# Attention and MLP in one kernel: Q and K rows interleaved in DRAM, and steps of the evacuation in other slots

## The chip, the cores and the metric

The kernel runs on one NeuronCore of a Trainium2 chip. The metric is the device time of one execution in microseconds (us). Times below are of the kernel before the change unless the text says otherwise. Six names recur. PE is the matmul engine, PEld its weight loads, DVE the vector engine, ACT the scalar engine, POOL the GpSimd engine, and SP the engine whose queue issues every DMA of this kernel. Each of them works through its own list of instructions in order. An instruction that waits holds up everything behind it on the same engine.

## The reference

The input is one sequence of 2048 rows of 512 numbers. The rows are layer-normalized; the normalized rows feed an attention block of 32 heads of width 16 and a dense block of width 1792, and the two results are combined.

```python
xn = _layernorm(x, axis=-1)
# A: attention, H = 32 heads, Dh = 16
q, k, v = (xn @ wqkv).reshape(B, S, 3, H, Dh) ...
scores = jnp.einsum("bhqd,bhkd->bhqk", q, k) * (Dh ** -0.5)
o = jnp.einsum("bhqk,bhkd->bhqd", _softmax(scores, axis=-1), v)
s = o.transpose(0, 2, 1, 3).reshape(B, S, D) @ wo
# B: dense, F = 1792
r = jnp.where(h > 0, h, 0)        # h = xn @ w1 + b1
b = (r * r) @ w2 + b2
return x + s * _silu(b)
```

Most products are made from numbers split in a high and a low part, three partial products each (high-high, high-low, low-high), so that the result keeps more bits than one pass would.

## The kernel before

**Lead-in (0 to about 196 us).** The rows are loaded, normalized and transposed. The Q, K and V projections run on PE. Q and K go out to DRAM tiles `q_d` and `k_d` of shape `[2, 128, 2048]`: index 0 of the first axis holds the high parts of 128 rows (8 heads of 16), index 1 the low parts. They come back later in another arrangement. For one head, 48 partitions of a tile `qe`, `qm` or `ka` hold three groups of 16 rows, for Q high, high, low and for K high, low, high, so that one matmul over 48 rows adds the three partial products. Each group is one DMA: three loads a head, for two heads (`j`) a tile.

**The loop.** Everything else is a loop of 512 slots. A unit is 16 slots: 4 heads and 512 queries. Unit u owns slots 16u to 16u+15, and in slot `st` PE computes the scores of 128 keys for the 4 heads of its unit (L1256, tile `se`), ACT takes the exponent (L1262, tile `pt`), and two slots later PE multiplies the exponents with V into the bank `po` (L373, 8 weight loads a slot; the last V column is 1, so that row 16 of each head is the sum). Rows `po L373` of the trace thus count the slots.

**The maxima.** The exponents need a shift for each query. Ahead of its use, the kernel computes the scores of a later unit once more (L300, tile `pm_t`, from `qm`), and DVE takes the maximum of each bank (L308): 2048 such reductions, 64 a unit. When a unit has all its maxima, `max_end` reduces them (L326), and `shift` negates them and splits the result: L336 makes the high part, L337 the low part, L341 transposes. The result goes to DRAM (`keep`, L344) and from there into two rows of the `qe` tiles (`back`, L364). From unit 16 on this happens about 7 slots ahead of the unit that needs it.

**The evacuation of a unit.** When a unit's `po` is complete, in slot 16u+17, ACT copies it to `ot`, and six steps follow at the slot distances of the table `EVAC` (`EVAC_LAST` for the last units): `evac_sums` (SP, loads the four rows of sums into a small tile `sm`), `evac_recip` (DVE, L397), `evac_keep` (SP, to DRAM `r_d`), `evac_back` (SP, broadcast back to `hl`), `evac_norm` (POOL, three operations, L411 to L413), `evac_store` (SP, four DMAs to `on_d`).

**The dense work.** PE has room beside the scores. A generator `dense` hands out its items a slot, or a block of four slots (`long_slots`), at a time: the MLP in 8 chunks of 256 rows (`mlp_tasks`: `first`, `first_pair`, `second`), then the output projection (`wo_part`) in blocks of 128 rows `(c, tt)`, four slots each, in the order `WO_ORDER`. Blocks of the columns c = 2 and 3 of the sequence, which wait for the last two units, are computed without those and finished at the very end (`unit_inner`, `unit_final`, `fill_mms`, `run_fill`). The tile `oc` holds the attention output that a column of blocks reads; `wo_load` and `wo_load_last` fill it.

**What sets the order.** Inside the loop the order on ACT, DVE, POOL, SP and PE is the order in which the Python code emits the instructions. `begin(st)` emits what is due in a slot: loads of K and V for the next four heads, loads of `qe` for the next unit, and then everything that `later(n, ...)` had put off to this slot. Loads of `qm` are emitted by `max_end` at steps counted in maxima (16 steps a unit).

Of the kernel before, what the change touches and what calls it, by code (L numbers as in the profile page):

```python
# [16 lines left out]
P = 128  # L17
# [17 lines left out]
EVAC = (1, 4, 5, 7, 9, 12)  # L35
EVAC_LAST = (1, 3, 4, 5, 7, 9)
# [4 lines left out]
def kernel(  # L41
# [16 lines left out]
    q_d = [dram.tile([2, P, S], F32, name=f"q_d{m}") for m in range(4)]  # L58
    k_d = [dram.tile([2, P, S], F32, name=f"k_d{m}") for m in range(4)]
# [12 lines left out]
    nc.vector.memset(eps_t, EPS)  # L72
    b1_t = const.tile([P, FO], F32, name="b1_t")
# [22 lines left out]
    with ExitStack() as ph:  # L96
# [33 lines left out]
        def load_head(t, j, src_d, h, parts, cols):  # L130
            for n, i in enumerate(parts):
                nc.sync.dma_start(  # L132
                    t[64 * j + DH * n : 64 * j + DH * (n + 1), :].bitcast(F32),
                    src_d[h // 8][i, (h % 8) * DH : (h % 8 + 1) * DH, cols],
                )

        def load_k(qd, n):

            p, j, i = n // 6, n // 3 % 2, n % 3
            if n % 6 == 0:  # L140
                kas[qd, p] = ring("ka")
            h = 4 * qd + 2 * p + j
            nc.sync.dma_start(
                kas[qd, p][64 * j + DH * i : 64 * j + DH * (i + 1), :].bitcast(F32),
                k_d[h // 8][i % 2, (h % 8) * DH : (h % 8 + 1) * DH, :],
            )
# [20 lines left out]
        def load_q_pair(u, name, p, tiles):  # L167
                qd, qc = divmod(u, 4)
                t = ring(name)
                for j in range(2):  # L170
                    load_head(
                        t, j, q_d, 4 * qd + 2 * p + j, (0, 0, 1), slice(qc * 512, (qc + 1) * 512)
                    )
# [140 lines left out]
        def max_end():  # L314
            while steps[0] < sum(done_m) // 4:
# [6 lines left out]
                if s in (9, 11) and u + 1 < NU:  # L322
                    load_q_pair(u + 1, "qm", (s - 9) // 2, qms.setdefault(u + 1, []))
# [10 lines left out]
        def shift(u):  # L334
            sh = sp.tile([P, 2, 16], F32R, name="sh")
            nc.vector.tensor_scalar(sh[:, 0], mxs[u], -1.0, None, op0=ALU.mult)  # L336
# [14 lines left out]
            if in_loop:  # L351
                later(1, keep)
                later(max(2, 16 * u - 14 - now[0]), back)
            else:
# [3 lines left out]
                else:  # L358
                    waiting.append((16 * u - 14, back))
# [19 lines left out]
        def evac(po, u):  # L379
# [4 lines left out]
            steps = EVAC_LAST if u >= 28 else EVAC  # L384
# [40 lines left out]
        def mlp_tasks(mp):  # L425
# [7 lines left out]
            rp = m1.enter_context(tc.tile_pool(name="rp", bufs=1))  # L433
# [119 lines left out]
            def second(c, tt):  # L553
# [86 lines left out]
        def wo_setup():  # L640
            wp = right(wstk, "wop", 1)
            st = right(wstk, "wo_st", 2)
# [6 lines left out]
            for ko in range(KO):  # L649
                later(3 * ko, lambda ko=ko: load(ko))  # L650
            wos["w"] = wot

# [843 lines left out]
```

## Time and profile before

| | us |
|---|---|
| median of 3 runs | 1661.2 (1657.56 to 1661.68) |
| the profiled execution | 1662.81 |
| its span | 1661.0 |
| lead-in, to the first `po` of the loop | about 196 |
| loop and tail | about 1465 |

Busy shares of the span: PE 98%, DVE 81%, ACT 72%, PEld 59%, POOL 31%. A busy PE does not mean that it is at its peak: matmuls overlap and their ends are modelled. The chain of waits, followed back from the last instruction, lies on PE for 93%. So the profile is best read slot by slot: two neighbouring slots of the same make-up take the same time to about 0.05 us, and a slot that is longer than its like shows a wait.

### The profile page before, as it was taken

The numbers are of one execution on the slowest core, as the hardware profiler recorded it, in microseconds if no ns is written. First come the engines' busy times: TensorE is split into PE (matmuls) and PEld (weight loads), VectorE is DVE, ScalarE is ACT, GpSimd is POOL, SyncE is SP. The second block draws the span as 40 slices with busy tenths as digits, with TensorE's granted clock in tenths as the row PEclk, the third lists the DMA queues.
The fourth block names the chain that finished last, engine by engine and source line by source line (L and its number), as shares of the span: only waits on it lengthen the run. The fifth ranks groups of instructions, "written<-read, shape, count | busy, mean of one in ns | idle before, by whom it ended". The sixth has DMA issues, their size and how long they took to land.

```text
span 1661.0 us, 35806 instructions
## 1 busy us (share of the span) xinstructions
PE 1625.6 (98%) x13642; PEld 983.6 (59%) x13642; DVE 1349.1 (81%) x2332; ACT 1187.8 (72%) x2344; POOL 510.9 (31%) x533
## 2 busy tenths in 40 slices
PE   6999999999999999999999999999999999998998
PEld 4899666456656665665565456555655565544455
DVE  6499888888887788877888888888888888887833
ACT  6221487678877887887787777777777777776784
POOL 4435567513212221231133113201321224113224
PEclk9999999999999999999999999999999999999999
DMA  8677555426332522353243324342332442144344
GB/s 285 168 227 251 176 173 165 124 65 175 85 91 74 164 74 81 101 138 73 78 122 98 92 72 140 93 109 72 116 98 71 106 127 73 45 117 128 124 134 140
DMA packets 155924, 201.22 MB, mean 121 GB/s; under 512 B 54824, under 2 KB 73768, under 8 KB 154216
## 3 DMA queue, kind: packets, MB, share of 16 engines
q1 hardware_dynamic: 155752, 198.93, 41.1%
q8 instruction: 108, 1.77, 0.4%
q14 instruction: 64, 0.52, 0.1%
HBM read 144.58 MB, written 53.99 MB: 120 GB/s over the span
## 4 chain that ended last, share of the span: by engine, by line
PE 93%; DVE 3%; DMA 2%; SPq 1%; ACT 0%; issue 0%; POOL 0%; DVEq 0%; ACTq 0%
PE po L373 29%; PE pm_t L300 16%; PE pd_t L234 16%; PE se L1256 15%; PE pd_t L202 5%; PE se L1014 3%; DVE mx L308 2%; PE se L965 2%; PE pd_t L773 2%; PE pd_t L1014 1%; PE po L1014 1%; SPq L132 1%; DMA sm<-ot 0%; DMA xc<-xn_d 0%; DMA xt<-in_A_x_dram 0%; PE pm_t L807 0%
## 5 line engine op out<-in xcount | busy, mean ns | idle before, releaser
L308 DVE TENSOR_REDUCE mx<-pm_t 128x1 f32<-128x512 f32 x2048 | 1265.4, 682 | 220.3 <-PE pm_t L300 120.8
L1262 ACT ACTIVATE pt<-se 128x512 f32<-128x512 f32 x1750 | 928.1, 613 | 234.7 <-PE se L1256 152.6
L300 PE MATMUL pm_t<-ka,qm 64*128 64x512 f32 x2048 | 783.1, 418 | 12.4 <-DVE mx L308 11.2
L1256 PE MATMUL se<-qe,ka 64*128 64x512 f32 x2016 | 745.0, 415 | 0.1
L373 PE MATMUL po<-pt,v 128*32 128x512 f32 x3564 | 525.3, 603 | 0.0
L300 PEld LDWEIGHTS pm_t<-ka,qm 64*128 64x128 f32 x2048 | 359.9, 184 | 227.0 <-DVE mx L308 214.0
L1256 PEld LDWEIGHTS se<-qe,ka 64*128 64x128 f32 x2016 | 353.3, 184 | 113.2 <-ACT pt L1262 74.1
L234 PEld LDWEIGHTS pd_t<-xc,w1s 64*128 64x128 f32 x2352 | 296.1, 187 | 44.2 <-issue 41.9
L234 PE MATMUL pd_t<-xc,w1s 64*128 64x256 f32 x2352 | 322.0, 286 | 0.0
L234 PE MATMUL pd_t<-w2t,hT 64*128 64x512 f32 x936 | 254.3, 407 | 0.0
L373 PE MATMUL po<-ex,v 128*32 128x512 f32 x532 | 213.2, 602 | 0.0
L1262 ACT ACTIVATE ex<-se 128x512 f32<-128x512 f32 x266 | 159.0, 614 | 43.2 <-PE se L1256 22.4
L234 PEld LDWEIGHTS pd_t<-w2t,hT 64*128 64x128 f32 x936 | 159.7, 184 | 43.6 <-issue 35.2
L373 PEld LDWEIGHTS po<-pt,v 128*32 128x32 f32 x3564 | 89.2, 108 | 160.4 <-issue 146.9
L547 POOL TENSOR_TENSOR r<-r 128x512 f32<-128x512 f32 x49 | 51.0, 1041 | 322.6 <-ACT r L544 322.6
L566 POOL TENSOR_TENSOR u<-u,b_t 128x512 f32<-128x512 f32 x16 | 20.6, 1287 | 286.6 <-ACT u L565 286.6
L202 PE MATMUL pd_t<-w2t,hT 64*128 64x512 f32 x408 | 106.3, 392 | 1.6 <-POOL w2t L81 0.8
L411 POOL TENSOR_TENSOR ot<-ot,hl 128x512 f32<-128x512 f32 x31 | 39.9, 1286 | 220.9 <-DMA hl<-r_d 148.2
L202 PEld LDWEIGHTS pd_t<-w2t,hT 64*128 64x128 f32 x408 | 72.4, 184 | 11.6 <-POOL w2t L80 1.2
L773 PE MATMUL pd_t<-wot,oc 64*128 64x512 f32 x258 | 74.5, 411 | 0.0
L81 POOL TENSOR_TENSOR hT<-r,hT 128x512 fp32r<-128x512 f32 x56 | 72.3, 1291 | 4.7
L1014 PE MATMUL se<-xT,wr_t 64*128 64x512 f32 x312 | 65.9, 390 | 0.0
(130 smaller groups left out, 1202.7 us busy)
## 6 DMA issues: line engine op xcount, KB each, us to landing
w1s<-w_d SPq DMA_DIRECT2D x196, 256.0 KB
qm<-q_d SPq DMA_DIRECT2D x384, 32.0 KB
qe<-q_d SPq DMA_DIRECT2D x384, 32.0 KB
ka<-k_d SPq DMA_DIRECT2D x96, 128.0 KB
xn_d<-xT SPq DMA_DIRECT2D x8, 1024.0 KB
k_d<-hl SPq DMA_DIRECT2D x32, 256.0 KB
q_d<-hl SPq DMA_DIRECT2D x32, 256.0 KB
xc<-xn_d SPq DMA_DIRECT2D x16, 512.0 KB
```

The lines of the kernel that those rows point to most:

```text
L81: (lo or nc.gpsimd).tensor_tensor(dst[1], raw, dst[0].bitcast(F32), op=ALU.subtract)
L202: mm = nc.tensor.matmul(out_, lh(r), rh(r), start=first_ and lane == 0, stop=last_ and lane == 1, skip_group_check=True,)
L234: mm = nc.tensor.matmul(out_, lh(r), rh(r), start=first_ and lane == 0, stop=last_ and lane == 1, skip_group_check=True,)
L300: nc.tensor.matmul(ps, qms[u][p][64 * j : 64 * j + 64, qb * P : (qb + 1) * P], kas[qd, p][64 * j : 64 * j + 64, kc * 512 : (kc + 1) * 512] ...
L308: return nc.vector.tensor_reduce(mxs[u][:, c, kc : kc + 1], ps, axis=AX.X, op=ALU.max)
L373: nc.tensor.matmul(po[32 * j : 32 * j + 32, :], vs[qd][:, (4 * kb + j) * VW : (4 * kb + j) * VW + 32], pts[j], start=(kb == 0), stop=(kb = ...
L411: nc.gpsimd.tensor_tensor(ot, ot, hl[:, 1].bitcast(F32), op=ALU.mult)
L547: nc.gpsimd.tensor_tensor(r, r, r, op=ALU.mult)
L773: inst = nc.tensor.matmul(ps[lane], oc[r, a, n, ts_], wot[r, b, n], start=m == 0 and (lane == 0 or wide), stop=m == kos and (lane == 1 or ...
L1014: inst = nc.tensor.matmul(out_, lh(r), rh(r), start=first_ and lane == 0, stop=last_ and lane == 1, skip_group_check=True,)
L1256: nc.tensor.matmul(se, kas[qd, j // 2][b : b + 64, kb * P : (kb + 1) * P], qes[u][j // 2][b : b + 64, :], start=True, stop=True,)
L1262: return nc.scalar.activation(pts[j], se, AF.Exp, scale=0.25)
```

## The change

The order of rows in DRAM: `q_d` and `k_d` become `[128, 2, 2048]`, with the high and the low row of each of the 128 rows side by side (for K the low one first). Two groups of a head are then 32 neighbouring rows, and one DMA loads them; a second DMA loads the remaining 16 rows. A store of Q is one DMA in place of two.

Other slots: `EVAC` and `EVAC_LAST` have new distances, and `EVAC_LAST` holds from unit 26 on; the first `qm` pair of a unit is asked for at step 3 in place of 9; the `qe` pairs of unit u in slots 16u-11 and 16u-10 in place of 16u-16 and 16u-15; the shift rows of units whose maxima are early, in slot 16u-9 in place of 16u-14; K loads one a slot over 8 slots in place of two a slot over 6; `gate` of the MLP one slot later.

The negation L336 becomes a `scalar_tensor_tensor` with a tile of zeros as its second tensor.

The output projection begins in slot 452 in place of 456: four slots that carried no dense work are gone. The tile for its first column is loaded ahead, while the MLP ends, and is used again for column 1. One more block, (3, 2), moves from the tail into the loop, so that the blocks from (0, 0) on keep their slots.

```diff
-EVAC = (1, 4, 5, 7, 9, 12)
-EVAC_LAST = (1, 3, 4, 5, 7, 9)
+EVAC = (1, 5, 6, 8, 12, 15)
+EVAC_LAST = (1, 4, 5, 6, 8, 10)
...
-    q_d = [dram.tile([2, P, S], F32, name=f"q_d{m}") for m in range(4)]
-    k_d = [dram.tile([2, P, S], F32, name=f"k_d{m}") for m in range(4)]
+    q_d = [dram.tile([P, 2, S], F32, name=f"q_d{m}") for m in range(4)]
+    k_d = [dram.tile([P, 2, S], F32, name=f"k_d{m}") for m in range(4)]
...
-        def load_head(t, j, src_d, h, parts, cols):
-            for n, i in enumerate(parts):
+        def load_head(t, j, src_d, h, hi, cols, both):
+            r = slice((h % 8) * DH, (h % 8 + 1) * DH)
+            if both:
                 nc.sync.dma_start(
-                    t[64 * j + DH * n : 64 * j + DH * (n + 1), :].bitcast(F32),
-                    src_d[h // 8][i, (h % 8) * DH : (h % 8 + 1) * DH, cols],
+                    t[64 * j : 64 * j + 2 * DH, :].bitcast(F32),
+                    src_d[h // 8][r, :, cols].rearrange("r i n -> (r i) n"),
                 )
+            else:
+                nc.sync.dma_start(
+                    t[64 * j + 2 * DH : 64 * j + 3 * DH, :].bitcast(F32),
+                    src_d[h // 8][r, hi, cols],
+                )
...
-                if s in (9, 11) and u + 1 < NU:
-                    load_q_pair(u + 1, "qm", (s - 9) // 2, qms.setdefault(u + 1, []))
+                if s in (3, 11) and u + 1 < NU:
+                    load_q_pair(u + 1, "qm", s // 11, qms.setdefault(u + 1, []))
...
-            nc.vector.tensor_scalar(sh[:, 0], mxs[u], -1.0, None, op0=ALU.mult)
+            nc.vector.scalar_tensor_tensor(
+                sh[:, 0], mxs[u], -1.0, zero, op0=ALU.mult, op1=ALU.add
+            )
...
-                later(max(2, 16 * u - 14 - now[0]), back)
+                later(max(2, 16 * u - 9 - now[0]), back)
...
-            steps = EVAC_LAST if u >= 28 else EVAC
+            steps = EVAC_LAST if u >= 26 else EVAC
...
-                    later(2, gate)
+                    later(3, gate)
...
             wos["w"] = wot
+            wos["oc", 2] = right(wstk, "oc2p", 1).tile([P, 2, KO, 512], F32R, name="oc2")
+            later(13, lambda: wo_load(2))
+            later(21, lambda: wo_load_last(2))
...
         WO_ORDER = (
-            [(2, t) for t in range(4)] + [(3, 0), (3, 1)]
+            [(2, t) for t in range(4)] + [(3, t) for t in range(3)]
...
-            for tt in (2, 3):
-                ps = tail["ps", tt] = free_ps["w"][tt - 2]
+            for tt in (3,):
+                ps = tail["ps", tt] = free_ps["w"][0]
...
-            wo_load(2)
-            later(1, lambda: wo_load_last(2))
             wo_ask(0)
             wo_ask(1)
-            for _ in range(4):
-                yield [], None
...
-            if st >= 64 and st % 64 < 6 and st // 64 + 1 < NQ:
-                for n in range(2):
-                    load_k(st // 64 + 1, 2 * (st % 64) + n)
+            if st >= 64 and st % 64 < 8 and st // 64 + 1 < NQ:
+                load_k(st // 64 + 1, st % 64)
             u, s = divmod(st + 16, 16)
-            if 2 <= u < NU and s < 2:
-                load_q_pair(u, "qe", s, qes.setdefault(u, []))
+            if 2 <= u < NU and s in (5, 6):
+                load_q_pair(u, "qe", s - 5, qes.setdefault(u, []))
...
-        run_fill(8)
+        run_fill(1)
         tail["out"](3)
-        run_fill(5)
```

What the change moves on the engines is shown at three places. Line numbers of the changed kernel are 2 to 13 higher; the numbers behind tile names are buffers.

The first place is SP's queue at the start of unit 29, slots 464 to 467, before: `on_d<-hl` is the store of unit 27, `qe` and `qm` are the loads of queries, `sm<-ot` the sums of unit 28.

```order
L420 DMA on_d_132<-hl 16x2x512 x4
L132 DMA qe_685<-q_d_60 16x512 x6
L713 DMA g<-g_d 128x512
L718 DMA xr<-in_A_x_dram 128x512
L132 DMA qe_686<-q_d_60 16x512 x6
L132 DMA qm_201<-q_d_60 16x512 x6
L391 DMA sm<-ot 128x1x16
L132 DMA qm_199<-q_d_60 16x512 x6
```

The same place after the change, from the rows `g` and `xr` of slot 460 on.

```order
L722 DMA g<-g_d 128x512
L727 DMA xr<-in_A_x_dram 128x512
L707 DMA oc_21230<-on_d_132 64x2x512
L722 DMA g<-g_d 128x512
L727 DMA xr<-in_A_x_dram 128x512
L398 DMA sm<-ot 128x1x16
L135 DMA qm_201<-q_d_60 32x512
L140 DMA qm_201<-q_d_60 16x512
```

The 18 query loads that stood ahead of the sums are behind them or far ahead of them. On DVE the reciprocal that reads these sums stood behind 40 maxima of its unit:

```order
L341 STREAM_TRANSPOSE sq<-sh 128x32
L308 TENSOR_REDUCE mx<-pm_t 128x1 x40
L397 RECIPROCAL sm<-sm 128x16
L308 TENSOR_REDUCE mx<-pm_t 128x1 x16
L326 TENSOR_REDUCE m_22195<-mx 128x16
```

and stands behind 45 now:

```order
L348 STREAM_TRANSPOSE sq<-sh 128x32
L313 TENSOR_REDUCE mx<-pm_t 128x1 x45
L404 RECIPROCAL sm<-sm 128x16
L313 TENSOR_REDUCE mx<-pm_t 128x1 x11
L331 TENSOR_REDUCE m_21927<-mx 128x16
```

The second place is POOL in the last MLP chunk, at the normalization of unit 24, before: `r` and `hT` are the square and the split of a `first_pair` block, `ot` and `hl` the normalization.

```order
L547 TENSOR_TENSOR r_2622<-r_2622 128x512
L80 TENSOR_SCALAR hT<-r_2622 128x512
L81 TENSOR_TENSOR hT<-r_2622,hT 128x512
L411 TENSOR_TENSOR ot<-ot,hl 128x512
L412 TENSOR_SCALAR hl<-ot 128x512
L413 TENSOR_TENSOR hl<-ot,hl 128x512
L547 TENSOR_TENSOR r_2623<-r_2623 128x512
```

After, the normalization stands one block later, behind the fourth in place of the third.

```order
L554 TENSOR_TENSOR r_2577<-r_2577 128x512
L82 TENSOR_SCALAR hT<-r_2577 128x512
L83 TENSOR_TENSOR hT<-r_2577,hT 128x512
L418 TENSOR_TENSOR ot<-ot,hl 128x512
L419 TENSOR_SCALAR hl<-ot 128x512
L420 TENSOR_TENSOR hl<-ot,hl 128x512
L554 TENSOR_TENSOR r_2576<-r_2576 128x512
```

The third place is the tail on PE, before: `se` are the last products of unit 30 (L855), `pm_t` the fill (L807), `po` the V product of slot 510.

```order
L855 MATMUL se<-w_21701,hl 128x512 x9
L807 MATMUL pm_t<-wot,oc 128x512 x8
L855 MATMUL se<-w_21701,hl 128x512 x3
L807 MATMUL pm_t<-wot,oc 128x512 x5
L373 MATMUL po<-pt_1499,v_1612 32x512
```

After:

```order
L865 MATMUL se<-w_21286,hl 128x512 x9
L817 MATMUL pm_t<-wot,oc_21230 128x512
L865 MATMUL se<-w_21286,hl 128x512 x3
L380 MATMUL po<-pt_1476,v_1592 32x512
L380 MATMUL po<-pt_1468,v_1592 32x512
```

Twelve fill matmuls are gone from it; the fill of the later steps (2, 4 and 5 matmuls) stays. In slots 452 to 455 PE has 21 half-row matmuls of block (2, 0) that were not there, and the maxima of these slots stand as 5, 3, 5, 3 in place of 4 a slot. Every other slot of the loop has the same instructions on PE.

More of the change, by code (lines that the diff above doesn't have):

```diff
@@ L687, in part @@
                 )
[L689 to L694 removed]
+            for ko in range(3):
+                later(ko, lambda ko=ko: part(ko, 0, 512))
         def wo_load_last(c):
@@ L724, in wo_part @@
         def wo_part():
-            for k in range(14):
+            for k in range(15):
                 c, tt = WO_ORDER[k]
```

86 lines of the change are left out of this document (43 added, 43 removed).

## The prediction

> **What bounds the kernel now.** I read first the page's busy shares and its chain by engine.
>
> ```profile
> PE 1625.6 (98%) x13642; PEld 983.6 (59%) x13642; DVE 1349.1 (81%) x2332; ACT 1187.8 (72%) x2344; POOL 510.9 (31%) x533
> PE 93%; DVE 3%; DMA 2%; SPq 1%; ACT 0%; issue 0%; POOL 0%; DVEq 0%; ACTq 0%
> ```
>
> PE carries 93% of the chain, and the change leaves PE's work as it is but for one block and twelve matmuls. What the many moved steps can bring lies in the other 7%, some 116 us. So I look for the slots that are longer than their like. The second view is the stretches of six units (columns: us from A to B, length, busy time of PE, PEld, DVE, ACT, POOL, then clock, DMA share, GB/s): units 1 and 2, 23 and 24, 28 and 29, each from its first `po` to the next unit's.
>
> ```profile
> 243.30:289.50 46.20, 46.20 (x432) 28.77 (x430) 40.40 (x70) 36.38 (x73) 33.56 (x42) 1.00 0.51 156
> 289.50:339.20 49.70, 47.19 (x354) 24.44 (x354) 41.93 (x70) 35.00 (x68) 23.28 (x24) 1.00 0.48 135
> 1239.50:1285.40 45.90, 45.90 (x358) 23.04 (x357) 40.49 (x70) 34.66 (x68) 6.40 (x6) 1.00 0.26 64
> 1285.40:1332.40 47.00, 46.28 (x404) 24.69 (x405) 40.35 (x70) 35.65 (x70) 9.32 (x9) 1.00 0.45 109
> 1470.50:1516.20 45.70, 44.45 (x328) 20.32 (x327) 40.97 (x71) 35.86 (x71) 14.97 (x15) 1.00 0.49 153
> 1516.20:1569.00 52.80, 47.86 (x342) 22.64 (x341) 40.41 (x70) 35.66 (x70) 13.42 (x11) 0.94 0.41 125
> ```
>
> Unit 29 is 7.1 us longer than unit 28, unit 2 is 3.5 longer than unit 1, unit 24 is 1.1 longer than unit 23. DVE is busy for 40 to 41 us of 46 in all of them, so it has little to give when it is held up. The chain inside unit 29 says why:
>
> ```profile
> 1516.34 0.36 SPq L132
> ...
> 1518.60 1.66 SPq L132
> ...
> 1523.09 0.02 SPq L391
> ...
> 1523.13 1.88 DMA sm<-ot
> ...
> 1525.10 0.25 DVE sm L397
> ...
> 1525.95 0.79 PE pm_t L300
> ```
>
> and SP's queue there what it was busy with (start, length, line, tile, count):
>
> ```profile
> 1507.68 2.14 SPq L420 DMA_DIRECT2D on_d<-hl  x4
> 1510.67 4.62 SPq L132 DMA_DIRECT2D qe<-q_d  x6
> ...
> 1516.34 3.91 SPq L132 DMA_DIRECT2D qe<-q_d  x6
> 1520.30 2.73 SPq L132 DMA_DIRECT2D qm<-q_d  x6
> 1523.13 0.60 SPq L391 DMA_DIRECT2D sm<-ot  x1
> 1523.83 2.73 SPq L132 DMA_DIRECT2D qm<-q_d  x6
> ```
>
> The sums were issued at 1523.13, behind 18 query loads. The reciprocal stands in DVE's list at a fixed place, waits for them, and holds the maxima behind it; their banks stay full, and PE waits (its granted clock also falls to 0.94 in this stretch). Unit 24 has the same wait, smaller:
>
> ```profile
> 1288.67 5.33 DMA sm<-ot
> ```
>
> In unit 2 the late guest of SP's queue is a piece of `w2`, behind twelve `qe` loads; then the negation L336 takes 1.19 us in place of its usual time:
>
> ```profile
> 287.78 0.61 SPq L132
> ...
> 291.14 3.56 DMA ex<-in_B_w_dram
> ...
> 295.48 1.28 POOL w2t L81
> ...
> 296.80 0.49 PE pd_t L202
> ...
> 301.48 1.19 DVE sh L336
> ```
>
> **The change, part by part.** *Fewer loads.* A head's three loads become two: `qe` and `qm` 384 to 256 each, `ka` 96 to 64, and Q's 32 stores become 16: 306 issues fewer. At 2.73 / 6 = 0.46 us an issue that is 140 us of SP's queue, and by itself nothing of the end, since SP's waits reach PE only through the three places above. Bytes and row lengths stay (2 KB and 8 KB). A load of 32 rows in place of 16 may land later; a unit's queries are asked for at least 10 slots (29 us at 46/16 = 2.9 us a slot) ahead, so I take 0.
>
> *Sums and reciprocal in units 24 and 29.* The 12 `qe` loads leave the start of the unit, where the first had waited for PE to be done with the tile, for its slots 5 and 6, as 8. Of the `qm` loads the first pair goes some 6 slots earlier. Sums keep their slot, the reciprocal comes one slot later. So the sums can be issued when ACT has copied `ot`, three slots ahead of their reader: 8.6 us, against the 5.33 us of the worst landing above. Nothing else is late on this path, so the whole excess goes: 7.1 + 1.1 = **8.2 us gained**. The bounds are 0 (something else holds the queue) and 8.2; I take the upper, for the chain names nothing else.
>
> *Unit 2.* The twelve `qe` loads around the `xc` load leave; `w2` comes 3 us (6 x 0.46) earlier, more than the 2.3 us (3.5 - 1.2) that the block waited. But eight `qe` loads now stand between the later pieces of `w2`, 8 x 0.46 = 3.7 us of queue, with four shift rows behind them. Bounds: 3.5 gained, and 1 lost if the later pieces come late as the first did. I take **1.5 gained**.
>
> *The negation and its neighbour.* Five rows first, two units: L336 began while POOL's L413 ran and ended when that ended; L337 did the same with L412.
>
> ```profile
> 891.44 1.17 DVE L336 TENSOR_SCALAR sh<-m 128x16 fp32r<-128x16 f32 x1
> 892.64 0.18 DVE L337 SCALAR_TENSOR_TENSOR sh<-m,sh 128x16 fp32r<-128x16 f32 x1
> ...
> 1167.98 0.49 DVE L337 SCALAR_TENSOR_TENSOR sh<-m,sh 128x16 fp32r<-128x16 f32 x1
> ```
> ```profile
> 891.29 1.29 POOL L413 TENSOR_TENSOR hl<-ot,hl 128x512 fp32r<-128x512 f32 x1
> ...
> 1167.84 0.62 POOL L412 TENSOR_SCALAR hl<-ot 128x512 fp32r<-128x512 f32 x1
> ```
>
> 891.44 + 1.17 and 891.29 + 1.29 both give 892.6; 1167.98 + 0.49 and 1167.84 + 0.62 both give 1168.5. Where nothing ran on POOL, L337 took 0.18. Busy time of L336 and then of L337 from 870 to 1600, the stretch in which DVE is tight:
>
> ```profile
> 870.00:1600.00 730.00, 5.93 (x16) 1.00 0.36 101
> 870.00:1600.00 730.00, 4.91 (x16) 1.00 0.36 101
> ```
>
> Sixteen of each undisturbed would be 16 x 0.17 + 16 x 0.18 = 5.6; so 10.84 - 5.6 = 5.2 us are waits for POOL. The new L336 has the form of L337, two tensors in SBUF, and L337's row shows that this form waits as well: I take 0 for the form itself (bounds: 3.2 gained, 16 x 0.1 lost). [...]
>
> *The normalization's slot* is what can move this wait. It comes three slots later (before: slot 10 of the unit, and the shift is due at 9 to 10). In units that run `first_pair` blocks, POOL's list now has another block's square and split ahead of it, so it cannot run before about slot 12: there the collisions go (units 15 and 21, in which the rows above lie, are such), about half of the 5.2. In units that run `second`, POOL is free and starts when `hl` lands; the reciprocal, and with it `hl`, is a slot later than before, which brings the last of POOL's three operations nearer to the shift. There I expect about 1 us more in all. Net **1.8 gained**; bounds 5.2 gained, and lost 16 x 1.0 - 5.2 = 10.8 if every unit met a whole operation.
>
> *The tail.* Twelve fill matmuls leave PE's chain:
>
> ```profile
> 1639.42 2.27 PE se L855 x9
> 1641.68 1.86 PE pm_t L807 x8
> 1643.54 0.69 PE se L855 x3
> 1644.23 1.16 PE pm_t L807 x5
> ```
>
> At 1.16 / 5 = 0.23 each, 12 x 0.23 = **2.8 gained**. Their cover goes with them: the fourth `se` group needs a bank that DVE frees after the first; the chain shows no wait of that group now, 1.86 us behind the ninth matmul, and one fill of 0.23 stays between. I take no new wait; the other bound is 1 us.
>
> *Slots 452 to 455.* Starts of `po` in the chain, four slots with maxima alone and then four with a block:
>
> ```profile
> 1473.47 1.00 PE po L373 x8
> ...
> 1484.29 0.99 PE po L373 x8
> ...
> 1495.81 1.00 PE po L373 x8
> ```
>
> 11.52 - 10.82 = **0.7 lost**. The block brings one ACT copy and two POOL operations, beside other work there (POOL is busy 15 us of 46 in unit 28). Its tile is loaded 13 to 21 slots after the MLP's last `first_pair` block, which frees the memory; the next item of it that could be late is unit 26's part (a rival below).
>
> *Edits that I cost at nothing.* K loads one a slot: the first pair is complete by slot 4, and the maxima of these heads begin at slot 8. `gate` later: ACT's Tanh stands behind POOL's addition and can only wait less. `evac_store` later: its reader is the output projection alone. Lead-in: chain on PE and DVE, fewer loads leave it as it is.
>
> Sum: 8.2 + 1.5 + 1.8 + 2.8 - 0.7 = 13.6. The profiled execution took 1662.81 around a span of 1661.0, so it would take 1649.2; it lies 1.6 over the median of the runs, 1661.2, which becomes **1647.6**.
>
> **The rivals.** A measurement of this kernel can tell about 0.3%, 5 us, from no change.
>
> *The sums are still late.* Other things stand ahead of them in unit 29 (`g`, `xr`, a part of `oc`), and some of these wait for POOL. If so, the 8.2 stay: 1655.8. Against it: in the rows above the queue was busy with query loads, 11.3 us of the time from 1510.67 to 1523.13. Chance 0.08, half of it on each side of the bound.
>
> *POOL's normalization meets the shift in every unit.* 12.6 us more than forecast (10.8 lost in place of 1.8 gained): 1660.2, no change. For it: in the `second` units nothing but the landing of `hl` holds POOL. Against it: the shift's two instructions last 0.35 us, POOL's chain 3.2. Chance 0.08.
>
> *Slower: block (2, 0) waits for unit 26.* Its last three matmuls need rows that unit 26 stores and slot 445 loads. Before, unit 27's store went out at 1507.68, 37 us after its evacuation began with unit 28 at 1470.5. The same delay for unit 26, whose evacuation began near 1425, gives 1462, the load behind it 1467, and slot 452 is at 1476: 9 us to spare. Each slot beyond that costs 2.9 us. It decides the sign from 14 + 9 = 23 us of further delay on; with 30 it gives 1647.6 + 21 = 1668.6. Chance 0.05.
>
> *All collisions go*, in unit 2 too: 5.2 and 3.5 in place of 1.8 and 1.5 give 1642.2. Chance 0.12.
>
> *The form frees L336.* Then L337, right behind it, meets the same operation of POOL; little changes, at most 1 us, and I count it with the forecast.
>
> **How the numbers follow.** The forecast has 0.67, with its own range 1642 to 1653 from the bounds of unit 2 (2 up, 2.5 down) and of the normalization (3.4 up, some 3 down). Faster by over 0.3%: 0.67 + 0.12 + 0.04 = 0.83; within 0.3%: 0.08 + 0.04 = 0.12; slower: 0.05. The range 1640 to 1657 leaves out the slower case, the one without change, and little at the lower end.
>
> **What would show it.** Unit 29 no longer than 46 us, with no wait of the reciprocal for `sm`, and the sums issued by its second slot. Unit 2 nearer to 47 than to 49.7. L341 of the changed file (the negation) with durations over 0.3 where POOL runs, fewer of them. From the ninth `se` matmul of the tail to the next `po` 0.9 us in place of 3.7. The prediction is wrong if a new wait of DVE or PE appears at each unit, or if the long slots of unit 29 stay.

## The result, and the profile after

The changed kernel takes 1646.8 us (median of 4 runs, 1646.45 to 1647.18) against 1659.9 before: a ratio of 0.992, with an interval of 0.9905 to 0.9939. The forecast was 1647.6. The profiled execution took 1647.18 around a span of 1645.4, 15.6 us less than the one before (1662.81); the profile of before lay 2.9 above its median, so a sum over the two profiles comes out 2 to 3 us larger than the difference of the medians.

The page's busy line and chain of the changed kernel:

```profile
PE 1619.7 (98%) x13651; PEld 983.2 (60%) x13651; DVE 1344.3 (82%) x2333; ACT 1186.7 (72%) x2345; POOL 513.0 (31%) x535
PE 96%; DVE 2%; DMA 1%; ACT 0%; issue 0%; SPq 0%; DVEq 0%; ACTq 0%
```

PE rose from 93% to 96% of the chain, and SP's queue fell from 1% to 0%. The same stretches as before, units 1 and 2, 23 and 24, 28 and 29 (columns as there):

```profile
244.20:290.50 46.30, 46.30 (x432) 28.76 (x430) 40.46 (x70) 36.42 (x73) 35.51 (x45) 1.00 0.57 176
290.50:337.60 47.10, 46.61 (x356) 24.53 (x355) 41.24 (x70) 34.74 (x68) 21.44 (x22) 1.00 0.44 114
1234.50:1280.20 45.70, 45.70 (x354) 22.89 (x352) 40.34 (x70) 34.53 (x68) 6.41 (x6) 1.00 0.31 80
1280.20:1325.90 45.70, 45.70 (x400) 24.95 (x398) 40.51 (x70) 35.14 (x70) 9.34 (x9) 1.00 0.38 97
1463.70:1510.80 47.10, 47.05 (x349) 23.04 (x348) 41.17 (x71) 36.29 (x72) 17.51 (x17) 1.00 0.49 144
1510.80:1556.30 45.50, 45.50 (x342) 21.60 (x341) 40.42 (x70) 35.45 (x70) 13.45 (x11) 1.00 0.39 119
```

Unit 29 fell from 52.8 to 45.5, unit 24 from 47.0 to 45.7, unit 2 from 49.7 to 47.1. Unit 28 became longer, 45.7 to 47.1. In unit 29 the sums (L398) now go out at 1509.27, before the unit's first `po` at 1510.8, and DVE reaches their reciprocal (L404) 8 us later without a wait. SP's rows first, then DVE's:

```profile
1506.17 0.38 SPq L727 DMA_DIRECT2D xr<-in_A_x_dram  x1
1509.27 0.60 SPq L398 DMA_DIRECT2D sm<-ot  x1
1509.96 0.43 SPq L135 DMA_DIRECT2D qm<-q_d  x1
```
```profile
1514.48 3.08 DVE L313 TENSOR_REDUCE mx<-pm_t 128x1 f32<-128x512 f32 x5 [0.20 <-PE pd_t L783]
1517.48 0.24 DVE L404 RECIPROCAL sm<-sm 128x16 f32<-128x16 f32 x1
```

Busy time of the negation L341 and of its neighbour L344 (the columns are DVE's busy time, clock, DMA share, GB/s):

```profile
870.00:1590.00 720.00, 3.00 (x16) 1.00 0.37 103
870.00:1590.00 720.00, 4.14 (x16) 1.00 0.37 103
```

That is 7.1 in place of 10.8; by the prediction's estimate of 5.6 for the undisturbed work, the waits for POOL went from 5.2 to 1.5 us. The tail, in the chain:

```profile
1626.63 2.29 PE se L865 x9
1628.92 0.23 PE pm_t L817
1629.15 0.69 PE se L865 x3
1629.84 1.85 PE po L380 x16
```

From the ninth `se` to the next `po` it is 0.92 us, 3.7 before.

If the starts of `po` of both traces are laid beside each other slot by slot, the 15.6 us split as follows (some 0.3 us lost are spread over other slots):

| | us |
|---|---|
| unit 29, unit 24 | -7.3, -1.3 |
| tail | -2.8 |
| unit 2 | -2.6 |
| slots with the shift, units 9 to 26 | -2.8 |
| first slot of a chunk, units 7, 10, 14 | -1.4 |
| slots 450 to 455, where the WO blocks begin | +0.8 |
| end of unit 28, where the scores of unit 29 begin and need its shift rows | +0.5 |
| lead-in and units 0 and 1 | +1.0 |

### The profile page after: what moved, and what is told of

Read it like the earlier page. It is cut to its first block, busy times and chain, and to the rows that moved or that the text cites. A ratio compares the mean times of both kernels' runs of the same rounds, so it can differ in the third digit from the quotient of the medians.

```text
span 1645.4 us, 35414 instructions
## 1 busy us (share of the span) xinstructions
PE 1619.7 (98%) x13651; PEld 983.2 (60%) x13651; DVE 1344.3 (82%) x2333; ACT 1186.7 (72%) x2345; POOL 513.0 (31%) x535
## 4 chain that ended last, share of the span: by engine, by line
PE 96%; DVE 2%; DMA 1%; ACT 0%; issue 0%; SPq 0%; DVEq 0%; ACTq 0%
PE po L380 30%; PE pd_t L239 17%; PE pm_t L305 16%; PE se L1269 16%; PE pd_t L207 6%; PE se L1027 3%; PE pd_t L783 2%; PE se L978 2%; DVE mx L313 1%; PE pd_t L1027 1%; PE po L1027 1%; DMA wv<-in_A_wqkv_dram 0%; DMA xc<-xn_d 0%; PE pm_t L1269 0%; DMA xt<-in_A_x_dram 0%; ACT xn L1076 0%
## 5 line engine op out<-in xcount | busy, mean ns | idle before, releaser
L783 PE MATMUL pd_t<-wot,oc 64*128 64x512 f32 x279 | 79.0, 406 | 0.0
L418 POOL TENSOR_TENSOR ot<-ot,hl 128x512 f32<-128x512 f32 x31 | 40.0, 1289 | 96.5 <-DMA hl<-r_d 47.9
```

The source lines that it names most:

```text
L418: nc.gpsimd.tensor_tensor(ot, ot, hl[:, 1].bitcast(F32), op=ALU.mult)
L783: inst = nc.tensor.matmul(ps[lane], oc[r, a, n, ts_], wot[r, b, n], start=m == 0 and (lane == 0 or wide), stop=m == kos and (lane == 1 or ...
```

## The experiments

A unit's time is always that from its first `po` to the next unit's, in the profiled execution: one execution of each kernel. Where the code of a unit is the same, it still moves: unit 24 of the kernel before took 47.0, and 46.0 in the kernel in which only a number of units 28 and later is changed, since DVE waited there 1.05 us for its sums in place of 1.97. The times of all kernels:

| kernel | median us | ratio to before, interval | unit 2 | 24 | 28 | 29 |
|---|---|---|---|---|---|---|
| before | 1660 | 1 | 49.7 | 47.0 | 45.7 | 52.8 |
| after | 1646.8 | 0.992, 0.9905 to 0.9939 | 47.1 | 45.7 | 47.1 | 45.5 |
| before, new query slots | 1662.5 | 1.001, 0.9999 to 1.0022 | 52.6 | 45.8 | 47.1 | 46.4 |
| before, new tables | 1649.9 | 0.994, 0.9912 to 0.9959 | 47.5 | 46.9 | 45.7 | 45.6 |
| before, one reciprocal later | 1655.6 | 0.997, 0.9958 to 0.9984 | 49.9 | 46.0 | 45.9 | 48.0 |
| before, new form | 1662.4 | 1.0016, 1.0004 to 1.0028 | 50.0 | 47.1 | 46.0 | 53.0 |
| after, old query slots | 1646.0 | 0.991, 0.9893 to 0.9932 | 47.6 | 45.7 | 46.6 | 45.5 |
| after, old tables | 1648.6 | 0.993, 0.9905 to 0.9948 | 48.1 | 46.7 | 46.7 | 45.5 |
| after, three loads | 1649.5 | 0.9935, 0.9915 to 0.9954 | 46.1 | 45.7 | 48.3 | 45.6 |
| after, early gate | 1647.3 | 0.992, 0.9908 to 0.9939 | 47.2 | 45.7 | 46.6 | 45.5 |
| after, tail fill | 1652.2 | 0.995, 0.9932 to 0.9971 | 47.0 | 45.7 | 47.3 | 45.5 |
| after, forced waits | 1663.6 | 1.001, 0.9998 to 1.0029 | 46.5 | 45.7 | 56.7 | 47.2 |
| best slots | 1645.9 | 0.991, 0.9891 to 0.9926 | 46.4 | 45.7 | 46.8 | 45.5 |
| best slots, `xc` first | 1646.6 | 0.991, 0.9895 to 0.9933 | 46.2 | 45.7 | 47.2 | 45.5 |

### Which part frees unit 29: the query loads or the tables

Four kernels, each with one part of the change alone or undone. The query slots, added to the kernel before or taken from the changed one; the shift rows move with them, from slot 16u-14 to 16u-9 (two lines left out here):

```diff
-                if s in (9, 11) and u + 1 < NU:
-                    load_q_pair(u + 1, "qm", (s - 9) // 2, qms.setdefault(u + 1, []))
+                if s in (3, 11) and u + 1 < NU:
+                    load_q_pair(u + 1, "qm", s // 11, qms.setdefault(u + 1, []))
...
-            if 2 <= u < NU and s < 2:
-                load_q_pair(u, "qe", s, qes.setdefault(u, []))
+            if 2 <= u < NU and s in (5, 6):
+                load_q_pair(u, "qe", s - 5, qes.setdefault(u, []))
```

> The kernel before with one part of the change alone: qe loads in slots 16u-11 and 16u-10, the first qm pair at step 3, the shift rows at 16u-9; three loads a head, old tables. Theory A: with the query loads away from the unit's start the sums are issued in time, so unit 29 falls from 52.8 to about 46 and unit 24 to 45.9: 8 us; unit 2, where w2 is no longer behind qe loads, gains 2: in all 1650. Rival B (fewer issues or the later reciprocal are needed too): unit 29 stays above 49, 1654 or more.

> The changed kernel, but the qe loads stand in slots 16u-16 and 16u-15 again, the first qm pair at step 9, the shift rows at 16u-14; still two loads a head, and the new evacuation tables. Theory A (the number of issues ahead of the sums and the slot of the reciprocal decide in unit 29): 8 query loads stand ahead of the sums of unit 28 in place of 18 before, so these go out 10 x 0.46 = 4.6 us earlier than before and the reciprocal comes a slot (2.9 us) later; 4.6 + 2.9 is more than the 7.1 us that unit 29 was too long, so unit 29 stays within 1 us of its 45.5, and unit 2 gets back some 1 us since w2 is behind 8 loads; in all 1647 to 1649. Rival B (the new slots of the query loads carry the gain): unit 29 is 50 us or longer, unit 24 46.5 or longer, unit 2 above 48.5; in all 1653 or more.

The evacuation tables, in the same way (taken from the changed kernel, the numbers alone):

```diff
-EVAC = (1, 4, 5, 7, 9, 12)
-EVAC_LAST = (1, 3, 4, 5, 7, 9)
+EVAC = (1, 5, 6, 8, 12, 15)
+EVAC_LAST = (1, 4, 5, 6, 8, 10)
...
-            steps = EVAC_LAST if u >= 28 else EVAC
+            steps = EVAC_LAST if u >= 26 else EVAC
```

> The kernel before with the new evacuation tables alone, the second from unit 26 on. Theory A: the sums are still issued behind 18 query loads, the reciprocal comes one slot (2.9 us) later: unit 29 keeps some 4 of its 7.1 us too many, unit 24 loses its 1.1; the collisions of the normalization with the shift go down by 2.6: in all 6 to 7 us faster, 1653 to 1654. Rival B (the reciprocal's slot is worth nothing, what is late is late by more): 1657. Rival C (it is the reciprocal's slot that carries the gain): unit 29 below 46.5, 1650 or less.

> The changed kernel with the numbers of both evacuation tables as before (the second table still holds from unit 26 on). Theory A: the sums are early enough for the old slot of the reciprocal too, so units 24 and 29 stay at 45.5 to 46; the normalization comes back to the slots where it met the shift, so the slots with the shift in units 15 to 26 lose the 2.6 us that they had gained; in all 1649 to 1650, with POOL's waits of the negation and its neighbour (busy 7.1 us now from 870 to 1590) back at 10 or more. Rival B (the reciprocal's slot was needed): unit 29 3 us longer as well, 1652 or more. Rival C (the collisions went for another reason, such as the form of the negation): no change, 1647.

The tables alone bring 10.2 us of the 13; the query slots alone bring nothing (1662.5); without them the changed kernel is as fast as with them (1646.0). Yet each of the two, alone, takes unit 29 down: to 46.4 with the query slots, to 45.6 with the tables. They are two cures for one wait, and either is enough. Of the expectations, neither fits the query slots alone: unit 29 fell as theory A had it, and the total did not. For the tables alone rival C came true, with 45.6 and 1649.9.

With the tables alone the sums still stand behind query loads. SP's rows there (the view begins at 1510 and so counts four of the six `qe` loads), and the stretch of unit 29:

```profile
1509.66 1.81 SPq L132 DMA_DIRECT2D qe<-q_d  x4
1511.51 3.78 SPq L132 DMA_DIRECT2D qm<-q_d  x6
1515.39 0.59 SPq L391 DMA_DIRECT2D sm<-ot  x1
```
```profile
1510.80:1556.40 45.60, 45.60 (x346) 21.84 (x346) 40.55 (x70) 35.55 (x70) 13.52 (x11) 1.00 0.45 133
```

The sums go out 4.6 us after the first `po`, in place of 6.9 before: unit 27 follows the second table too, its store (four issues) leaves two slots earlier, and so it does not stand in the queue at this place. The reciprocal comes 2.9 us later. 2.3 + 2.9 = 5.2 us, and the wait of 5.41 is gone. In units 16 and 24, which follow the first table, DVE still waits for the sums, for 2.13 and 1.37 us, and PE loses 2.0 and 1.3 (units 16 and 24 take 47.9 and 46.9): there the query loads do have to go.

With the query slots alone, three loads a head and the old tables, the twelve `qe` loads stand in the middle of the unit, ahead of other guests of SP's queue. The stretches of units 1 and 2, and the chain in unit 2:

```profile
242.60:291.10 48.50, 46.95 (x433) 28.85 (x431) 40.82 (x70) 36.59 (x73) 31.99 (x41) 1.00 0.50 158
291.10:343.70 52.60, 49.57 (x353) 25.44 (x352) 40.74 (x70) 35.10 (x68) 24.88 (x26) 0.94 0.41 111
```
```profile
305.62 0.42 SPq L132
...
309.15 6.78 DMA hl<-r_d
316.10 1.27 POOL ot L411
317.45 0.64 POOL hl L412
...
319.42 0.60 POOL w2t L80
```

`hl` lands late, the normalization stands in POOL's list ahead of the pieces of `w2`, and the blocks wait for these. Units 1 and 2 lose 5.3 us, unit 28 loses 1.4, units 16 and 22 lose 0.7 each: together 8.1, a little more than the 7.6 that units 24 and 29 had brought. A part of the loss in unit 2 is PE's granted clock, 0.94 in that stretch: it was 0.50 for 6.8 us from 322.0 on.

With the old numbers in the changed kernel, units 15 to 27 lose 1.3 us net, and the negation and its neighbour are busy 5.08 + 4.22 = 9.3 us in place of 7.1. Unit 24 is 1.0 longer, from one negation of 1.17 us beside POOL; the sums are not waited for. So the collisions do come with the slot of the normalization, though less than the 2.6 that I expected.

### One number of the table

```diff
-EVAC_LAST = (1, 3, 4, 5, 7, 9)
+EVAC_LAST = (1, 4, 4, 5, 7, 9)
```

> The kernel before with one number changed: the reciprocal of the last units (28 on) one slot later, 4 in place of 3. Theory A (place in the list counts slot by slot): of the 5.41 us that DVE waited for the sums in unit 29, 2.9 go, and the remaining 2.5 are too short for the half clock (6.83 us at 0.50 in unit 29 of the kernel before), so unit 29 takes 47 to 48.5 in place of 52.8; 5 us faster in all. Rival B (it was the store of unit 27, two slots earlier by the rule that the second table holds from unit 26 on, that freed the queue): unit 29 stays at 50 or more.

DVE's row of the reciprocal in unit 29, in the kernel before and then in this one, and the stretch:

```profile
1525.10 0.25 DVE L397 RECIPROCAL sm<-sm 128x16 f32<-128x16 f32 x1 [5.41 <-DMA sm<-ot]
1524.30 0.25 DVE L397 RECIPROCAL sm<-sm 128x16 f32<-128x16 f32 x1 [2.39 <-DMA sm<-ot]
```
```profile
1515.20:1563.20 48.00, 46.20 (x346) 21.49 (x345) 41.10 (x70) 35.81 (x70) 13.51 (x11) 1.00 0.46 139
```

The wait fell from 5.41 to 2.39, the unit from 52.8 to 48.0, and its clock is 1.00. That 2.5 us would be too short for the half clock was my estimate; none followed the 2.39 us here, and in the next experiment 3.4 us of it followed a wait of 2.55. One number moves 4.5 us of the median. Slot by slot, against the changed kernel, the wait costs PE 1.7 us; another 0.85 of this unit is a negation that took 1.01 us beside POOL (at 1537.22; the kernel before had no such meeting there). So the loss by the wait fell from 7.3 to 1.7, by 5.6, with 3.0 us of wait: 2.6 us must be something else. The next experiment asks whether it is the clock.

### What a wait costs PE

In unit 29 of the kernel before, PE's stretches (columns: us, PE busy, granted clock, DMA share, GB/s) around the wait read:

```profile
1520.50:1523.90 3.40, 0.52 (x6) 1.00 0.24 68
1523.90:1530.70 6.80, 4.75 (x20) 0.50 0.45 132
```

The clock was 0.50 for 6.8 us. To see whether the wait does this, the changed kernel got waits of three sizes:

```diff
-                later(n, lambda fn=fn: fn(u, ev))
+                if not (fn is evac_recip and 26 <= u < 29):
+                    later(n, lambda fn=fn: fn(u, ev))
...
-            nc.sync.dma_start(
-                ev["sm"], ev["ot"].rearrange("(j r) (a b) -> j r a b", r=32, b=16)[:, DH]
-            )
+            for _ in range({27: 2, 28: 3}.get(u, 1)):
+                nc.sync.dma_start(
+                    ev["sm"], ev["ot"].rearrange("(j r) (a b) -> j r a b", r=32, b=16)[:, DH]
+                )
+            if 26 <= u < 29:
+                evac_recip(u, ev)
```

> The changed kernel, with the reciprocal of units 26, 27 and 28 put right behind the load of the sums, and this load made once, twice and three times in a row (each waits for the one ahead, some 2.3 us each). So DVE waits in units 27, 28 and 29 for about 2, 4.5 and 7 us. Theory A (a long wait of PE brings the granted clock to 0.50 for 3.41 or 6.83 us, and this is part of what unit 29 lost): unit 27 gets 1 to 2 us longer at clock 1.00, unit 29 some 6 by the wait and 2 to 3 more by the clock, with a stretch at 0.50 behind the wait; unit 28 lies at the border. Rival B (the clock fell in unit 29 for another reason): no stretch at 0.50 in units 27 to 29, each longer by its wait alone.

DVE's rows of the three reciprocals, and PE before and in the slow stretch behind each:

```profile
1418.05 0.25 DVE L408 RECIPROCAL sm<-sm 128x16 f32<-128x16 f32 x1 [2.55 <-DMA sm<-ot]
1469.52 0.25 DVE L408 RECIPROCAL sm<-sm 128x16 f32<-128x16 f32 x1 [4.40 <-DMA sm<-ot]
1524.90 0.25 DVE L408 RECIPROCAL sm<-sm 128x16 f32<-128x16 f32 x1 [6.85 <-DMA sm<-ot]
```
```profile
1415.60:1419.00 3.40, 1.32 (x14) 1.00 0.14 39
1419.00:1422.40 3.40, 3.40 (x16) 0.50 0.58 175
1466.80:1470.20 3.40, 0.05 (x2) 1.00 0.16 39
1470.20:1477.00 6.80, 6.63 (x27) 0.50 0.06 14
1518.00:1521.40 3.40, 1.38 (x12) 1.00 0.52 142
1521.40:1531.60 10.20, 5.85 (x21) 0.50 0.40 112
```

The slot starts against those of the changed kernel give what each cost, with some waits of a reciprocal from other traces:

| DVE's wait | PE at clock 0.50 | lost by PE |
|---|---|---|
| 1.37 (before, new tables, unit 24) | none | 1.3 |
| 1.97 (before, unit 24) | none | 1.3 |
| 2.13 (before, new tables, unit 16) | none | 2.0 |
| 2.39 (before, one reciprocal later) | none | 1.7 |
| 2.55 | 3.4 | 3.9 |
| 4.40 | 6.8 | 6.4 |
| 5.41 (before) | 6.8 | 7.3 |
| 6.27 (before, new form, unit 29) | 6.8 | 7.5 |
| 6.85 | 10.2 | 9.2 |

Theory A holds, and its smallest wait was a miss: I had expected clock 1.00 there, and the second, 4.40, "at the border"; where a border lies was my estimate, and half clock followed all three. In these runs the waits up to 2.39 us cost PE less than their own length (by 0.1 to 0.7 us), those from 2.55 us on cost 1.2 to 2.4 us more, and half clock followed each of these and none of the shorter. So of the 7.3 us of unit 29 some 2 to 2.6 were the clock (an estimate: 7.3 - 5.4 at the least; 2.6 if the wait alone would have cost 0.7 less than its length, as that of 2.39 did).

The spread of the runs goes with the clock as well: of 23 runs of the kernel before, the 17 with a mean clock of 0.996 or 0.997 take 1661.6 us on average, the 6 with 0.998 or 0.999 take 1658.2.

### The other edits

*The form of the negation*, alone in the kernel before:

```diff
-            nc.vector.tensor_scalar(sh[:, 0], mxs[u], -1.0, None, op0=ALU.mult)
+            nc.vector.scalar_tensor_tensor(
+                sh[:, 0], mxs[u], -1.0, zero, op0=ALU.mult, op1=ALU.add
+            )
...
```

> The kernel before with the new form of the negation alone (scalar_tensor_tensor with a tile of zeros). Theory A (as predicted: this form waits for POOL as the old one does): no change, 1660 +- 1, and the negation takes 0.5 to 1.2 us in the units 15, 16, 17, 21 and 26 as it did. Rival B (only the old form is held up): the negation takes 0.2 there, up to 3.2 us faster. Rival C (the two-tensor form is held up more often): up to 1.6 slower.

The new form, by its group (durations in ns: least, median, greatest):

```profile
L338 DVE SCALAR_TENSOR_TENSOR sh<-m,zero x32: 113/175/1154, 116.7 to 1585.6; 128x16 fp32r<-128x16 f32 x32
```

It is held up as the old one was, to 1154 ns (the old form to 1257). In single units it is longer or shorter (unit 14 0.94, unit 15 0.26 in place of 0.58 and 1.17; the expectation numbers these units one higher, by the unit that the shift is for), as POOL's operations happen to lie. It brings no gain. The median is 0.16% higher, about 2.4 us; the profile shows 0.5. The clock is a candidate for the rest: all ten runs have a mean of 0.996 or 0.997, and the profile has a stretch at 0.50 in unit 2 (3.4 us from 298.2 on, behind the wait for `w2`) that the kernel before has not. The kernel with one reciprocal later, which has the old form, has one at the same place (298.1), so this is not shown to come from the form.

*The gate.*

```diff
-                    later(3, gate)
+                    later(2, gate)
```

> The changed kernel with the gate of the MLP two slots after its post step again in place of three. Theory A (from the two traces: ACT's Tanh waited 0.90 us for POOL's addition, with the exponents behind it): the slots in which a chunk starts in units 7, 10, 13 and 14 are each some 0.5 us longer, in all 1.9: 1648.7. Rival B (as the prediction had it, the gate costs nothing): 1646.8, with these slots as they are now.

The first slots of a chunk in units 7, 10 and 14 get 0.46, 0.46 and 0.45 us longer, 1.4 in all; that of unit 13 does not. ACT's rows in unit 7 of this kernel and then of the changed one:

```profile
516.71 0.70 ACT L1275 ACTIVATE pt<-se 128x512 f32<-128x512 f32 x1
518.32 0.63 ACT L578 ACTIVATE r<-u 128x512 f32<-128x512 f32 x1 [0.91 <-POOL u L573]
518.86 3.02 ACT L1275 ACTIVATE pt<-se 128x512 f32<-128x512 f32 x6
```
```profile
517.52 0.70 ACT L1275 ACTIVATE pt<-se 128x512 f32<-128x512 f32 x1
519.13 3.10 ACT L1275 ACTIVATE pt<-se 128x512 f32<-128x512 f32 x6 [0.91 <-PE pm_t L305]
```

ACT is idle for 0.91 us at this place in both kernels; in the changed one it waits for PE. With the early gate the Tanh (L578) could not use this gap, since it waited for POOL, and starts when it ends: the six exponents start 0.54 us behind the Tanh. So what PE loses is not the 0.91 but the Tanh's own time. The median (1647.3) is too coarse to tell 1.4 us; the slots are not.

The later gate has a price at another place, which the same run shows: with the early gate unit 28 is 0.5 shorter. In both kernels SP's queue stands behind the gate's last operation on POOL (L580). In the changed one this ends at 1476.6, 0.5 us behind the start of slot 452, and the shift rows of unit 29 go out 1.1 us ahead of the slot that they delay (1499.97 against 1501.11); with the early gate it ends 2.4 us ahead of slot 452, and they go out 3.6 us ahead.

*Two loads of 16 rows in place of one of 32:*

```diff
-                nc.sync.dma_start(
-                    t[64 * j : 64 * j + 2 * DH, :].bitcast(F32),
-                    src_d[h // 8][r, :, cols].rearrange("r i n -> (r i) n"),
-                )
+                for i in range(2):
+                    nc.sync.dma_start(
+                        t[64 * j + DH * i : 64 * j + DH * (i + 1), :].bitcast(F32),
+                        src_d[h // 8][r, i, cols],
+                    )
```

> The changed kernel with the interleaved rows, but with the 32 rows of a load fetched as two loads of 16, so three loads a head again, in the new slots. Theory A (as predicted, the number of loads is worth nothing by itself): units 24 and 29 stay at 45.5 to 46, in all within 1 us of 1646.8. Rival B (the queue is short of room for 306 issues more): sums or shift rows late again, 3 us or more lost.

Units 24 and 29 stay. Unit 28 takes 48.3 in place of 47.1, as the shift rows of unit 29 go out later, at 1502.01, just behind the start of the slot that they delay (1501.90). Unit 0 took 50.1 in place of 47.8, by the clock: 0.50 for 3.4 us from 203.0 on, behind a wait for `xc`. The kernel with the extra fill shows the same in unit 0 (49.4), where its code is that of the changed kernel, so this can't be put down to the loads. The 1.2 us in unit 28 can, as far as one execution shows: in the kernels with the changed kernel's loads and query slots, the forced waits apart, this unit took 46.6 to 47.3.

*The fill of the tail:*

```diff
+                for n in range(12):
+                    fill.append(lambda ps=ps, ts_=ts_: nc.tensor.matmul(
+                        ps, oc[:, 0, 0, ts_], wot[:, 0, 0], start=True, stop=False,
+                        skip_group_check=True,
+                    ))
...
-        run_fill(1)
+        run_fill(8)
         tail["out"](3)
+        run_fill(5)
```

> The changed kernel with twelve extra fill matmuls in the tail at the places where they stood before (8 behind the ninth se matmul, 4 with the one behind the twelfth); they write a bank that is started anew afterwards. Theory A (each lies on PE's chain): 12 x 0.23 = 2.8 us longer, 1649.6. Rival B (the fill stood in a wait that is there now, or the time has gone elsewhere): less than 1 us longer.

```profile
1629.47 2.29 PE se L870 x9
1631.76 1.85 PE pm_t L816 x8
1633.61 0.69 PE se L870 x3
1634.31 0.93 PE pm_t L816 x4
1635.23 0.23 PE pm_t L822
1635.47 1.85 PE po L380 x16
```

3.71 us from the ninth `se` to the next `po` in place of 0.92: 2.8, the forecast term. The median rose by 5.4, of which the profile finds 1.5 in unit 0 (the clock) and 0.5 in unit 20 beside it.

### Two versions from these results

```diff
-EVAC = (1, 5, 6, 8, 12, 15)
-EVAC_LAST = (1, 4, 5, 6, 8, 10)
+EVAC = (1, 4, 5, 7, 12, 15)
+EVAC_LAST = (1, 4, 5, 6, 8, 11)
...
-                later(3, lambda: split((wot[:, 0, ko], wot[:, 1, ko]), raw))
+                later(2, lambda: split((wot[:, 0, ko], wot[:, 1, ko]), raw))
```

> The changed kernel with the reciprocal of the first table, and what follows it but the normalization, one slot earlier (4, 5, 7; normalization and store stay at 12 and 15), the store of the second table at 11, and the split of the WO pieces one slot earlier. Theory: in units with second blocks the normalization ends a slot ahead of the shift, so the collisions of units 20 and 26 go (0.3 + 1.0), and the shift rows of unit 29 go out ahead of the store (0.5): 1.8 less, 1645. Rival: other collisions take their place, or the pieces wait in unit 2: no change within 1 us.

```diff
-            load_w1(0)
             load_xc(0)
-            for fo in (1, 2):
-                load_w1(fo)
+            load_w1(0)
             state["w"] = []
             split_w1(0)
-            later(1, lambda: [split_w1(1), load_w1(3)])
-            later(2, lambda: load_w1(4))
+            later(1, lambda: [load_w1(1), load_w1(2)])
+            later(2, lambda: [split_w1(1), load_w1(3), load_w1(4)])
```

> The kernel best_slots, and in the first slots of the loop the xc load is issued ahead of the first w1 load, two further w1 loads a slot later. Theory (in every run PE waits 1.4 us and more for xc in the first slots, and in two runs the clock fell to 0.50 for 3.41 us behind it, unit 0 taking 49.4 and 50.1 us in place of 45.9 to 47.8): xc, 1 MB, lands 1 to 2 us earlier, so unit 0 takes 46 and the clock doesn't fall there: 1 to 2 us less than best_slots, and less spread. Rival: the w1 piece, now behind xc, is what is late: no change or 1 us more.

In the first, units 20, 26 and 28 take 45.8, 46.0 and 46.8 in place of 46.2, 46.6 and 47.1, 1.3 us in all. That this comes from the new steps is not shown: the kernel with three loads, which has the changed kernel's own steps, has 45.9 and 46.0 in units 20 and 26, and the second version, which has the new ones, has 47.2 in unit 28. Its median is 0.9 under that of the changed kernel, which these runs can't tell from no difference. The second is no better: its rival came true, POOL waited 5.14 us, in place of 0.40, for the `w1` piece that now stood behind `xc`, and unit 0 took 48.6 in place of 46.8.

## Why the prediction was right, and where it was not

The median came out 0.8 us from the forecast, which is closer than the terms were. The terms were read from the profiles, and between the two profiles the gain was 15.6 in place of 13.6; the medians moved by 13.1, as the profile of before lay 2.9 above its median and not 1.6. That the two differences nearly cancel is luck. (The groups that the prediction lists for the 306 issues sum to 304; three fewer loads of `oc` and one more of `g` make up the rest. Nothing hangs on it.)

*Sums and reciprocal, 8.2 forecast, 8.6 measured.* The size was right, as the whole excess went. The reason was half right. I put it on the query loads, "for the chain names nothing else"; the runs show that the later reciprocal and the earlier store do the same in unit 29 without them, and that the query slots, on top of the other parts, are worth nothing that the median shows (1646.0 without). The chain named what stood in front of the sums, not the only way past it. I read the clock of 0.94 in that stretch and made nothing of it: it was some 2 to 2.6 of the 7.3 us. The 1.3 of unit 24 is less certain: DVE's wait there, 1.97, was 1.05 in another execution of the same code.

*Unit 2, 1.5 forecast, 2.6 measured.* The first wait for `w2` went, the later pieces were not late. What is left is one shift beside POOL (1.16 us of L344 in unit 2). The tables alone take the unit to 47.5 too, so here as well the query loads were not the only way past the wait. Why the tables do this there was not followed up.

*Form, 0 forecast.* Right: no gain (the form alone takes 1662.4, the kernel before 1660), and the negation is still held up, to 1154 ns there (the old form to 1257).

*Normalization, 1.8 forecast, 2.8 measured.* The collisions follow the slot of the normalization: L341 and L344 are busy for 7.1 us in place of 10.8, and for 9.3 with the old numbers. In the units with `first_pair` blocks the collisions are gone (units 15, 21, 22 and 25 gained 1.0, 0.3, 0.4 and 1.0). In all nine kernels with the normalization in the new slots these units take 45.7 to 45.9; in the five with the old slots they take 45.8 to 46.9, so how much is gained varies. In units with `second` blocks the normalization ends close to the shift and met it in two of them, for 0.47 us in unit 20 (as before) and for 1.22 in unit 26 (0.7 lost); unit 16 gained 0.4. I had put the loss in these units at 1 us; it was 0.3 net.

*Tail, 2.8 forecast, 2.8 measured*, and given back by the twelve matmuls to the same number.

*Slots 452 to 455, 0.7 lost forecast, 0.8 measured.*

*Edits costed at nothing.* This step failed twice. "ACT's Tanh stands behind POOL's addition and can only wait less" was right, and worth 1.4 us: what stands behind the Tanh are the exponents, and PE with them. The shift rows of unit 29 came 0.5 us late at the end of unit 28. This took two of the edits: with the rows back in slot 16u-14 (and the old query slots), or with the early gate, unit 28 is 0.5 shorter. Fewer loads are worth nothing in units 24 and 29 and about 1.2 us in unit 28.

No rival came true in the changed kernel. The one of the late sums has its place in the kernel with the tables alone, in units 16 and 24; and no rival had the clock: the five waits of 2.55 us and more, with half clock behind them, cost 1.2 to 2.4 us above their own length, the four shorter ones 0.1 to 0.7 less than theirs.

## What to carry to other kernels

A late DMA that an engine waits for, as DVE did here for 5.41 us, can be cured at both ends, by what stands ahead of it in the queue and by the place of its reader. Two edits that each cure it do not add up (unit 29 gained 6.4 us by the query slots, 7.2 by the tables, 7.3 by the whole change), and only a run with one of them shows which was needed. A slot-by-slot comparison of two traces finds effects of 0.5 us that medians with a spread of 2 us can't; but a trace is one execution, and the same unit of the same code moved by 1.0 us between two (unit 24, 47.0 and 46.0), so a small effect needs a second trace. An instruction that "can only wait less" is worth what stands behind it on its engine: here six exponents behind a Tanh, 1.4 us in units 7, 10 and 14.

## What the runs showed of the hardware

PE's granted clock has two values in these runs, 1.00 and 0.50, and it falls in stretches of 3.4 us or two or three times that (6.8 in unit 29 of the kernel before, 3.4, 6.8 and 10.2 behind the forced waits). In the loop it fell ten times, each time where PE had been busy for 0.05 to 1.86 of the 3.4 us ahead, a length taken from these stretches. Two near cases, first in the kernel with three loads a head (the clock fell right behind), then in the changed kernel (it did not), both at the wait for `xc`:

```profile
199.60:203.00 3.40, 1.86 (x19) 0.99 1.01 324
```
```profile
199.60:203.00 3.40, 2.04 (x23) 1.00 1.05 330
```

It is no sharp line: behind one such stretch with less work, that of the wait of 2.13 us in unit 16 of the kernel with the tables alone, the clock stayed at 1.00.

```profile
921.60:925.00 3.40, 1.75 (x18) 1.00 0.87 126
```

So the clock fell behind 1.86 us of work in 3.4 us and did not behind 1.75; what else decides is open. A wait of 2.1 us without any matmul, in the first of the forced waits, brought 3.4 us at half clock. PE did not have to be idle for all of the 3.4 us ahead: the clock fell behind stretches with 1.32, 1.38 and 1.86 us of work.
